# The first weight's scale is made behind its last decode, ahead of the first rows' transposes, with idle products in front of both

## The chip, the core and the metric

One core of a Trainium2 chip. The metric is the device time of one execution in microseconds, from runs of the whole program; a profiled execution comes with a trace of every instruction. Engines: PE (TensorE, products), PEld (its weight loads), DVE (VectorE), ACT (ScalarE), POOL (GpSimd), SP (SyncE, which issues the DMAs).

## The reference, cut to what matters

```
A  = softmax(q @ k_lm.T / 8);  Bm = softmax(q_lm @ k_lm.T / 8);  C = softmax(q_lm @ k.T / 8)
Z  = 6 Newton steps from Bm.T / (norm_1 * norm_inf):  Z = 2 Z - Z @ Bm @ Z
x  = A @ Z @ C @ v                      # 8 batches, 8 heads, 576 rows, head 64; 32 landmarks
u  = x + real(fft over rows and columns of x)          # per batch 576 x 512
un = (u - mean(u)) / sqrt(var(u) + 1e-6)
out = u + relu(un @ w_ch1) @ w_ch2       # w_ch1 512 x 2048, w_ch2 2048 x 512
```

## The kernel before

The last line of the reference is nearly all the work. Rows go through it in 18 chunks of two tiles of 128 rows. Both weights and the rows are held as pairs of half-precision numbers (a high and a low part), and each product takes three products of halves (`mm3`). In a chunk, eight steps multiply the transposed rows `unT` with two pieces of 128 columns of the first weight each (tile `h`, 24 products of 256 columns), ACT and DVE rectify and split the result, and eight `second` steps multiply that with the second weight into `acc` (12 products of 512 columns each).

Before this can begin, `weights` (line 275) makes the weights ready. They come as 64-bit numbers, in 16 pieces per weight (`NF = 16`), the first weight's ahead of the second's. Per piece: a DMA on SP's queue (`raw`); ACT takes the magnitudes (`prepare`, tile `row`); DVE or ACT takes the low bits and DVE puts both together (the decode, `w<-row,w`); PE adds the piece's squares to a gram matrix in the bank `acc1` (`squares`, four products). When all 16 are in, `scale` makes one power of two for the whole weight: DVE takes the gram matrix's diagonal (`wd`) and its sum (`wm`), PE spreads that over the partitions with a product against ones, DVE bounds it (`wp_e`), POOL raises it to the power -1/2 (`wp_r`), and DVE cuts and inverts it and writes the scale (`wsc`). Only then can `halve` split a piece into halves: ACT the high part, DVE the low part (both `w<-w,wsc`), two pieces after each decode (`PACE = 2`). In step i of the loop over the 32 pieces the squares of piece i - 2 are issued, so those of piece 15 come with decode 17, and `scale(0)` behind it (line 354). It takes one of the four `at` banks and waits in the plan until one is read out (`till(a2, banks=1)`). The second weight's scale comes behind decode 31.

The order of PE's instructions is made by a planner at build time. `run` (line 991) keeps a clock `now` and steps through threads: attention and mix of a batch first, then the weights, then the products of the chunks. Each thread says how long it wants to wait, from costs and due times that the kernel keeps for DVE, ACT and POOL. PE runs strictly in the planned order; while the plan has nothing for it and no chunk's second half has begun, it puts in idle products of 256 columns into `acc0` (`self.spare`, line 1015). The other engines' instructions are ordered by the compiler's scheduler, with the program's order as priority, and each of them runs its list in order.

The first batch's rows come out of `mix` (two tiles at a time) and go through `norm` (line 849): statistics, the power on POOL, the normalised rows (tile `row`), then, for the first four tiles, transposes on PE (line 248) into an `at` bank, and ACT and DVE split them into `unT`. In the plan before, the first two tiles' transposes and the second mix's products stand ahead of the first scale's product.

Of the kernel before, what the change touches and what calls it, by code (L numbers as in the profile page):

```python
# [10 lines left out]
F32 = mybir.dt.float32  # L11
# [7 lines left out]
P = 128  # L19
H, S, D, LM, DM, DF = 8, 576, 64, 32, 512, 2048  # L20
NF = DF // P
# [137 lines left out]
class Kernel:  # L159
# [80 lines left out]
    def mm(self, out, a, b, start=True, stop=True, share=1.0):  # L240
        self.there[out.name] = self.now
        self.now += share * (1.0e-3 if a.dtype == F32 else 0.42e-3) * math.prod(b.shape[1:])
        self.nc.tensor.matmul(out, a, b, start=start, stop=stop, skip_group_check=True)  # L243

    def tr(self, out, a, ident):
        self.there[out.name] = self.now
        self.now += 0.11
        self.nc.tensor.transpose(out, a, ident)  # L248
# [26 lines left out]
    def weights(self):  # L275
        nc = self.nc
        V, A = self.V, self.A
        whole = self.whole
        slots = [[t[:, OFF + 512 * i : OFF + 512 * i + 512] for i in range(NF)] for t in whole]
        upper = [[t.bitcast(BF16).rearrange("p (m x) -> p m x", x=2)[:, :, 1] for t in ss] for ss in slots]  # L280
        hl = [[t[:, 512 * i : 512 * i + 512].bitcast(F16).rearrange("p (y m) -> p y m", y=2) for i in range(NF)] for t in whole]
        self.w1s = [t.rearrange("p y (c f) -> p y c f", c=KT) for t in hl[0]]
        self.w2s = hl[1]
        sc = self.cp.tile([P, 3], F32, name="wsc")
        pieces = [(w, f) for w in range(2) for f in range(NF)]
        mags = []

        def prepare(i):


            mag = self.row(512)
            top = self.wraw[i].rearrange("p (m x) -> p m x", x=2)[:, :, 1].bitcast(F32)
            A.late = self.raw_there[i]
            A.activation(mag, top, AF.Prelu, scale=2.0**-112, alpha=-(2.0**32))
            mags.append(mag)

        def squares(i):

            w, f = pieces[i]
            for c in range(KT):  # L300
                x = upper[w][f][:, P * c : P * c + P]
                self.mm(self.gram[:, P * w : P * w + P], x, x, i == 0 and c == 0, f == NF - 1 and c == KT - 1)

        es = []

        def scale(w):

            dg, a2 = self.small(P, "wd"), self.small(1, "wm2")
            V.tensor_tensor(dg, self.gram[:, P * w : P * w + P], self.ident, ALU.mult)
            V.tensor_reduce(a2, dg, AX.X, ALU.add)  # L310
            yield self.till(a2, banks=1)
            ps = self.psum()
            self.mm(ps[:, 0:1], self.ones, a2)
            e, r = self.small(1, f"wp{w}_e"), self.small(1, f"wp{w}_r")
            V.tensor_scalar(e, ps[:, 0:1], 2.0**-120, 2.0**126, ALU.max, ALU.min)
            self.G.tensor_tensor(r, e, self.mhalf[:, 0:1], ALU.pow)
            V.tensor_scalar(r.bitcast(I32), r.bitcast(I32), 0x7F800000, None, ALU.bitwise_and)
            V.reciprocal(e, r)
            es.append(e)
            V.tensor_scalar(sc[:, w : w + 1], r, (2.0**12, 2.0**14)[w], None, ALU.mult)  # L320

        def halve():
            w, f = pieces[sum(self.split_w)]
            self.split(hl[w][f][:, 0], hl[w][f][:, 1], slots[w][f], sc[:, w : w + 1])
            self.split_w[w] = f + 1

        for i, (w, f) in enumerate(pieces):
            while len(mags) < min(2 * NF, i + 1 + PREP):
                j = len(mags)
                while len(self.wraw) < min(2 * NF, j + 1 + AHEAD):  # L330
                    self.raw()
                if self.raw_there[j] > self.now:
                    if j > i:
                        break
                    yield self.raw_there[j] - self.now
                    continue
                prepare(j)
            low = self.wraw[i].rearrange("p (m x) -> p m x", x=2)[:, :, 0]
            x, dst = mags[i].bitcast(I32), slots[w][f].bitcast(I32)
            (A if i % 2 else V).late = self.raw_there[i]  # L340
            if i % 2 == 0:
                V.tensor_scalar(dst, low, 29, None, ALU.logical_shift_right)
            else:
                byte = self.wraw[i].bitcast(mybir.dt.uint8).rearrange("p (m x) -> p m x", x=8)[:, :, 3]
                A.activation(dst, byte, AF.Copy, scale=2.0**-5, bias=-0.484375)
            V.scalar_tensor_tensor(dst, x, 3, dst, ALU.logical_shift_left, ALU.bitwise_or)
            if i > 1:
                squares(i - 2)
            self.decoded = i + 1
            if self.decoded == 2 * NF:  # L350
                self.load(1)
            yield max(0.0, max(self.V.free, self.G.free) - self.now - WT)
            if i == NF + 1:
                yield from scale(0)
            for _ in range(PACE if es else 0):
                if self.split_w[0] < NF:
                    halve()
                    yield max(0.0, max(self.V.free, self.G.free) - self.now - WT)
        squares(2 * NF - 2)
        yield 0.0  # L360
        squares(2 * NF - 1)
        yield from scale(1)
        V.tensor_scalar(sc[:, 2:3], es[0], 2.0**-25, es[1], ALU.mult, ALU.mult)
        self.inv2 = sc[:, 2:3]
        while sum(self.split_w) < 2 * NF:
            halve()
            yield max(0.0, max(self.V.free, self.A.free) - self.now - WT)
# [481 lines left out]
    def norm(self, b, uts):  # L849
        nc, V = self.nc, self.V  # L850
        n = len(uts)
# [29 lines left out]
        for j, ut in enumerate(uts):  # L881
            i = self.ntile
            while i // TCH >= self.first_done + NT - (1 < i // TCH < 4):
                yield 0.5
            self.ntile += 1
            self.utiles.append(ut)
            if i % TCH == 0:
                self.unT.append(
                    self.wk.tile([P, 1024], I32, name="unT", bufs=NT).bitcast(F16).rearrange("p (y c t) -> p y c t", y=2, c=KT)
                )  # L890
            unT = self.unT[-1]
            at = P * (i % TCH)
            if i < 2 * TCH:
                yield self.till(uns[j], banks=1) + (LATER if i >= TCH else 0.0)
                ps = self.psum()
                for c in range(KT):
                    self.tr(ps[:, P * c : P * c + P], uns[j][:, P * c : P * c + P], self.ident)
                self.split(*(unT[:, y, :, at : at + P] for y in range(2)), ps.rearrange("p (c t) -> p c t", c=KT), 1.0)
                self.ready.append(self.now + self.till(unT))
                yield 0.0  # L900
                continue
            hl = self.row(1024, F16).rearrange("p (y d) -> p y d", y=2)
            self.A.copy(hl[:, 0], uns[j])
            (self.G if b > 1 else V).tensor_tensor(hl[:, 1], uns[j], hl[:, 0], ALU.subtract)
            for y in range(2):
                nc.sync.dma_start_transpose(unT[:, y, :, at : at + P], hl[:, y])
            self.there[unT.name] = self.there[hl.name] + 4.0
            self.ready.append(self.now + self.till(unT))
            yield 0.0
# [81 lines left out]
    def run(self):  # L991


        self.ntile, self.utiles, self.unT, self.ready = 0, [], [], []
        self.ulive, self.ufree, self.first_done, self.seconds, self.folded = 0, [], 0, 0, -1
        self.split_w, self.decoded = [0, 0], 0
        self.threads = []
        self.spawn(self.attention(), 1)
        self.spawn(self.weights(), 2)
        self.spawn(self.mlp(), 3)  # L1000
        with self.tc.manual_schedule(engines={mybir.EngineType.PE}):
            while self.threads:
                for th in self.threads:
                    if th[1] <= self.now:
                        try:
                            wait = next(th[2])
                            th[1] = self.now + wait
                        except StopIteration:
                            self.threads.remove(th)
                        break  # L1010
                else:

                    until = min(t[1] for t in self.threads)
                    while self.spare is not None and until - self.now > 0.25:
                        self.mm(self.spare[:, 0:256], self.ones16, self.idle)
                    self.now = until
                assert self.now < 5000
# [67 lines left out]
```

## Time and profile before

| | us |
|---|---|
| median of three runs | 994.53 |
| lowest and highest | 993.15, 995.64 |
| the profiled execution | 993.68 |
| its span, first to last instruction | 991.9 |
| PE busy in it | 955.5 |
| DVE busy | 593.3 |
| ACT busy | 319.4 |
| mean granted TensorE clock | 0.986 |

Engines run at the same time, so the busy times don't add up. The weights are made ready and the first batch computed in the first 130 us; from there to the end PE multiplies rows with weights nearly without a pause. Where the profile gives only a helper's line (138 for DVE, ACT and POOL, 243 for products), the tiles' names tell operations apart.

### The profile page before, as it was taken

The numbers are of one execution on the slowest core, as the hardware profiler recorded it, in microseconds if no ns is written. First come the engines' busy times: TensorE is split into PE (matmuls) and PEld (weight loads), VectorE is DVE, ScalarE is ACT, GpSimd is POOL, SyncE is SP. The second block draws the span as 40 slices with busy tenths as digits, with TensorE's granted clock in tenths as the row PEclk, the third lists the DMA queues.
The fourth block names the chain that finished last, engine by engine and source line by source line (L and its number), as shares of the span: only waits on it lengthen the run. The fifth ranks groups of instructions, "written<-read, shape, count | busy, mean of one in ns | idle before, by whom it ended". The sixth has DMA issues, their size and how long they took to land.

```text
span 991.9 us, 20749 instructions
## 1 busy us (share of the span) xinstructions
PE 955.5 (96%) x8700; PEld 664.2 (67%) x8700; DVE 593.3 (60%) x1593; ACT 319.4 (32%) x652; POOL 119.0 (12%) x124
## 2 busy tenths in 40 slices
PE   6869999899999999999999999999999999999998
PEld 4648656667666777676666776676766777666665
DVE  7989797796467635396467736784634835141111
ACT  5559653243214322143214322432213412120110
POOL 0000000023021301032012301150110401010000
PEclk8889999999999999999999999999999999999999
DMA  9854204135121511025112321134111301020000
GB/s 332 292 212 150 65 2 172 37 59 154 49 44 42 149 55 23 22 58 154 44 44 42 99 104 43 23 61 172 22 33 33 52 1 42 16 40 22 1 22 22
DMA packets 97774, 74.66 MB, mean 75 GB/s; under 512 B 68112, under 2 KB 86544, under 8 KB 97552
## 3 DMA queue, kind: packets, MB, share of 16 engines
q1 hardware_dynamic: 97680, 73.34, 25.6%
q8 instruction: 68, 1.11, 0.5%
q14 instruction: 26, 0.21, 0.1%
HBM read 48.02 MB, written 9.44 MB: 58 GB/s over the span
## 4 chain that ended last, share of the span: by engine, by line
PE 86%; DVE 9%; DMA 2%; ACT 2%; issue 1%; POOL 0%; SPq 0%; DVEq 0%; ACTq 0%; POOLq 0%
PE h L243 36%; PE acc L243 35%; PE at L243 14%; DVE w L138 2%; DVE u L138 1%; DVE lm L138 1%; DVE mid L138 1%; DVE row L138 1%; DMA big<-k_dram 1%; PE at L248 1%; DMA big<-v_dram 1%; ACT w L138 0%; DMA out_dram<-u 0%; ACT row L138 0%; ACT mid L138 0%
## 5 line engine op out<-in xcount | busy, mean ns | idle before, releaser
L243 PE MATMUL h<-unT,w 128*128 128x256 f16 x3456 | 411.2, 273 | 3.8 <-DMA unT<-row 1.7
L243 PEld LDWEIGHTS <-w 128*128 128x128 f16 (+1 forms) x3584 | 344.9, 99 | 79.9 <-DVE w L138 7.3
L243 PE MATMUL acc<-w,h 128*128 128x512 f16 x1632 | 381.6, 380 | 2.7 <-DVE w L138 2.2
L243 PEld LDWEIGHTS <-h 128*128 128x128 f16 x1632 | 157.2, 99 | 162.6 <-issue 6.3
L138 DVE SCALAR_TENSOR_TENSOR h<-h 128x512 f16<-128x512 f32 x136 | 93.6, 688 | 224.8 <-ACT h L138 224.6
L138 ACT ACTIVATE h<-h 128x512 f16<-128x512 f32 x136 | 80.9, 595 | 321.8 <-PE h L243 315.7
L138 POOL TENSOR_TENSOR r<-ve,mhalf 128x2 f32<-128x2 f32 (+1 forms) x20 | 13.3, 667 | 476.6 <-DVE ve L138 472.2
L138 POOL TENSOR_TENSOR mid<-mid 128x640 f16<-128x640 f32 (+2 forms) x36 | 48.7, 1365 | 161.1 <-ACT mid L138 123.7
L138 DVE TENSOR_REDUCE lm<-big 128x32 f32<-128x576 f32 (+1 forms) x48 | 44.5, 940 | 2.8 <-DMA big<-k_dram 2.5
L243 PEld LDWEIGHTS <-big 128*128 128x128 f16 (+1 forms) x864 | 40.1, 103 | 8.1 <-issue 1.9
L138 ACT CAST row<-row 128x512 f16<-128x512 f32 (+1 forms) x40 | 20.8, 552 | 63.9 <-DVE row L138 63.9
L138 POOL TENSOR_TENSOR row<-row 128x512 f16<-128x512 f32 (+1 forms) x33 | 35.4, 1089 | 39.6 <-ACT row L138 37.7
L243 PEld LDWEIGHTS <-mid 64*128 64x128 f16 (+1 forms) x624 | 29.3, 95 | 14.8 <-issue 8.2
L138 DVE SCALAR_TENSOR_TENSOR u<-at,scw,w 128x128 f32<-128x128 f32 (+3 forms) x105 | 33.8, 389 | 5.8 <-PE at L243 4.1
L138 DVE SCALAR_TENSOR_TENSOR u<-acc,wsc,u 128x512 f32<-128x512 f32 x36 | 26.9, 748 | 12.3 <-PE acc L243 12.0
L138 DVE SCALAR_TENSOR_TENSOR w<-at,scw,w 128x262 f32<-128x262 f32 (+1 forms) x42 | 19.1, 485 | 25.2 <-ACT w L138 25.2
L243 PE MATMUL at<-mid,big 128*128 128x262 f16 (+1 forms) x288 | 32.6, 282 | 0.0
L138 DVE TENSOR_TENSOR E<-at,mask 128x256 f32<-128x256 f32 x48 | 20.1, 419 | 17.9 <-PE at L243 17.9
L243 PEld LDWEIGHTS at<-RE,E 128*128 128x128 f32 x192 | 26.6, 194 | 5.0 <-DVE big L138 1.6
L243 PE MATMUL at<-RE,E 128*128 128x64 f32 (+1 forms) x192 | 29.0, 275 | 0.2 <-DVE RE L138 0.2
L138 DVE SCALAR_TENSOR_TENSOR big<-big,aq_r 128x1024 f16<-128x1024 f32 (+1 forms) x32 | 26.8, 868 | 3.5 <-ACT big L138 3.5
L138 DVE TENSOR_TENSOR mid<-mid 128x256 f32<-128x256 f32 (+2 forms) x52 | 28.6, 584 | 0.0
(179 smaller groups left out, 897.8 us busy)
## 6 DMA issues: line engine op xcount, KB each, us to landing
w<-w_dram SPq DMA_DIRECT2D x22, 512.0 KB, 6.8
big<-v_dram SPq DMA_DIRECT2D x16, 640.0 KB, 9.5
big<-q_dram SPq DMA_DIRECT2D x16, 584.0 KB, 6.7
big<-k_dram SPq DMA_DIRECT2D x16, 576.0 KB, 5.4
out_dram<-u SPq DMA_DIRECT2D x36, 256.0 KB, 2.0
big<-w_dram SPq DMA_DIRECT2D x10, 512.0 KB, 6.5
t<-t_dram SPq DMA_DIRECT2D x1, 1048.0 KB, 10.7
unT<-row SPq DMA_TRANSPOSE x64, 2.4
```

The costliest lines, as they stand in the source:

```text
L138: ins = call(out, *args, **kw)
L243: self.nc.tensor.matmul(out, a, b, start=start, stop=stop, skip_group_check=True)
L248: self.nc.tensor.transpose(out, a, ident)
```

## The change

It adds `warm(n)`, which issues n idle products without moving the planner's clock. The squares of pieces 14 and 15 are issued right behind decode 15, with 24 idle products ahead of those of piece 15, and `scale(0)` follows at once, ahead of decode 16. Its product takes a bank of the `h` pool, its wait in the plan is only for the diagonal's sum, and eight idle products follow it. The transposes in `norm` are not issued before that (`self.scaled`). Decodes 16 and 17 no longer issue squares, and the splits begin behind piece 15. Nothing changes for the second weight's scale.

```diff
--- before.py
+++ after.py
@@ -242,6 +242,10 @@
         self.now += share * (1.0e-3 if a.dtype == F32 else 0.42e-3) * math.prod(b.shape[1:])
         self.nc.tensor.matmul(out, a, b, start=start, stop=stop, skip_group_check=True)
 
+    def warm(self, n):
+        for _ in range(n):
+            self.nc.tensor.matmul(self.spare[:, 0:256], self.ones16, self.idle, start=True, stop=True, skip_group_check=True)
+
     def tr(self, out, a, ident):
         self.there[out.name] = self.now
         self.now += 0.11
@@ -297,6 +301,8 @@
         def squares(i):
 
             w, f = pieces[i]
+            if i == NF - 1:
+                self.warm(24)
             for c in range(KT):
                 x = upper[w][f][:, P * c : P * c + P]
                 self.mm(self.gram[:, P * w : P * w + P], x, x, i == 0 and c == 0, f == NF - 1 and c == KT - 1)
@@ -308,9 +314,12 @@
             dg, a2 = self.small(P, "wd"), self.small(1, "wm2")
             V.tensor_tensor(dg, self.gram[:, P * w : P * w + P], self.ident, ALU.mult)
             V.tensor_reduce(a2, dg, AX.X, ALU.add)
-            yield self.till(a2, banks=1)
-            ps = self.psum()
+            yield self.till(a2, banks=1) if w else max(0.0, self.there[a2.name] - self.now)
+            ps = self.psum() if w else self.ps_h.tile([P, 512], F32, name="h")
             self.mm(ps[:, 0:1], self.ones, a2)
+            if w == 0:
+                self.warm(8)
+            self.scaled = True
             e, r = self.small(1, f"wp{w}_e"), self.small(1, f"wp{w}_r")
             V.tensor_scalar(e, ps[:, 0:1], 2.0**-120, 2.0**126, ALU.max, ALU.min)
             self.G.tensor_tensor(r, e, self.mhalf[:, 0:1], ALU.pow)
@@ -344,13 +353,16 @@
                 byte = self.wraw[i].bitcast(mybir.dt.uint8).rearrange("p (m x) -> p m x", x=8)[:, :, 3]
                 A.activation(dst, byte, AF.Copy, scale=2.0**-5, bias=-0.484375)
             V.scalar_tensor_tensor(dst, x, 3, dst, ALU.logical_shift_left, ALU.bitwise_or)
-            if i > 1:
+            if i > 1 and not NF <= i < NF + 2:
                 squares(i - 2)
             self.decoded = i + 1
             if self.decoded == 2 * NF:
                 self.load(1)
             yield max(0.0, max(self.V.free, self.G.free) - self.now - WT)
-            if i == NF + 1:
+            if i == NF - 1:
+                squares(NF - 2)
+                yield 0.0
+                squares(NF - 1)
                 yield from scale(0)
             for _ in range(PACE if es else 0):
                 if self.split_w[0] < NF:
@@ -890,6 +902,8 @@
                 )
             unT = self.unT[-1]
             at = P * (i % TCH)
+            while not self.scaled:
+                yield 0.1
             if i < 2 * TCH:
                 yield self.till(uns[j], banks=1) + (LATER if i >= TCH else 0.0)
                 ps = self.psum()
@@ -993,7 +1007,7 @@
 
         self.ntile, self.utiles, self.unT, self.ready = 0, [], [], []
         self.ulive, self.ufree, self.first_done, self.seconds, self.folded = 0, [], 0, 0, -1
-        self.split_w, self.decoded = [0, 0], 0
+        self.split_w, self.decoded, self.scaled = [0, 0], 0, False
         self.threads = []
         self.spawn(self.attention(), 1)
         self.spawn(self.weights(), 2)
```

## Rows read from the trace of the kernel before

**Rows 1.** From the page: busy time of each engine (share of the span) and instructions; the TensorE clock that was granted, in tenths, in 40 slices of 24.8 us; and one group of DMA issues (count, size of one, median us from issue to landing).

```profile
PE 955.5 (96%) x8700; PEld 664.2 (67%) x8700; DVE 593.3 (60%) x1593; ACT 319.4 (32%) x652; POOL 119.0 (12%) x124
...
PEclk8889999999999999999999999999999999999999
...
w<-w_dram SPq DMA_DIRECT2D x22, 512.0 KB, 6.8
```

**Rows 2.** Busy time by stretch (us from the span's start). Columns: stretch, its length, then busy us and instructions of PE, PEld, DVE, ACT and POOL, the granted TensorE clock, the mean busy share of the DMA engines, GB/s. The stretches were chosen around the change; the one from 62.1 overlaps others.

```profile
50.00:62.70 12.70, 7.77 (x100) 5.51 (x100) 11.82 (x30) 8.93 (x18) 0.02 (x1) 1.00 0.82 318
62.70:64.80 2.10, 0.00 (x0) 0.00 (x0) 2.03 (x8) 0.00 (x0) 0.69 (x1) 0.63 0.47 131
64.80:70.00 5.20, 5.16 (x25) 4.24 (x26) 2.67 (x5) 2.23 (x4) 0.00 (x0) 0.50 0.38 154
73.50:76.90 3.40, 3.40 (x21) 2.54 (x19) 3.03 (x8) 3.40 (x8) 0.00 (x0) 0.50 0.47 137
85.60:108.50 22.90, 22.09 (x233) 19.47 (x233) 21.14 (x38) 17.95 (x32) 0.00 (x0) 1.00 0.61 205
62.10:108.50 46.40, 40.98 (x385) 34.72 (x386) 39.86 (x88) 33.02 (x60) 1.96 (x3) 0.89 0.42 139
108.50:126.80 18.30, 16.00 (x95) 8.96 (x96) 14.90 (x26) 10.72 (x18) 0.55 (x1) 1.00 0.01 1
126.80:200.00 73.20, 69.11 (x703) 45.79 (x703) 57.66 (x176) 28.39 (x63) 3.87 (x5) 0.98 0.24 73
200.00:992.00 792.00, 785.97 (x6987) 541.63 (x6984) 426.87 (x1143) 210.74 (x435) 111.90 (x109) 1.00 0.21 55
```

**Rows 3.** PE in order of time, 50 to 130 us. Columns: start, us (from the first start to the last end of the merged products), engine, line, operation, out<-in, shapes, count, and in brackets the idle time before and what ended it. acc<-w are gram products, acc<-idle,ones idle products, h<-unT,w products of the rows with the split first weight, acc<-w,mid and acc<-w,h products with the split second weight.

```profile
53.61 1.52 PE L243 MATMUL at<-mid,big 128*128 128x262 f16 x12
...
62.18 0.40 PE L243 MATMUL acc<-w 128*128 128x128 bf16 x4 [2.77 <-DVE w L138]
...
64.84 1.94 PE L248 MATMUL at<-ident,row 128*128 128x128 f32 x8 [2.15 <-DVE row L138]
66.57 2.83 PE L243 MATMUL at<-mid,big 128*128 128x262 f16 x12
...
69.62 0.43 PE L243 MATMUL at<-wm,ones 128*128 128x1 f32 x2
...
73.24 3.39 PE L243 MATMUL h<-unT,w 128*128 128x256 f16 x16 [0.42 <-DVE w L138]
...
81.81 2.78 PE L243 MATMUL h<-unT,w 128*128 128x256 f16 x24
...
85.64 0.82 PE L243 MATMUL h<-unT,w 128*128 128x256 f16 x6 [0.82 <-DVE mid L138]
...
92.43 0.60 PE L248 MATMUL at<-ident,row 128*128 128x128 f32 x4
...
110.01 0.28 PE L243 MATMUL at<-wm,ones 128*128 128x1 f32 x2
...
126.78 3.59 PE L243 MATMUL acc<-w,h 128*128 128x512 f16 x11 [2.23 <-DVE w L138]
```

**Rows 4.** DVE in order of time, 60 to 81 us, the same columns. w<-row,w is a decode, wd and wm the gram matrix's diagonal and its sum, row<-u,mv,r the two row normalisations, unT<-at,unT the low part of a transposed row tile, wp_e the first reader of the scale's product, wsc the scale, w<-w,wsc the low part of a split.

```profile
61.46 0.66 DVE L138 SCALAR_TENSOR_TENSOR w<-row,w 128x512 int32<-128x512 int32 x1
...
63.57 0.28 DVE L138 TENSOR_REDUCE wm<-wd 128x1 f32<-128x128 f32 x1
...
64.14 1.00 DVE L138 TENSOR_SCALAR row<-u,mv,r 128x512 f32<-128x512 f32 x2
...
66.59 0.69 DVE L138 SCALAR_TENSOR_TENSOR unT<-at,unT 128x512 f16<-128x512 f32 x1 [0.51 <-ACT unT L138]
67.44 0.69 DVE L138 SCALAR_TENSOR_TENSOR unT<-at,unT 128x512 f16<-128x512 f32 x1 [0.16 <-ACT unT L138]
70.08 0.16 DVE L138 TENSOR_SCALAR wp_e<-at 128x1 f32<-128x1 f32 x1 [1.94 <-PE at L243]
...
71.47 0.14 DVE L138 TENSOR_SCALAR wsc<-wp_r 128x1 f32<-128x1 f32 x1
...
72.43 0.74 DVE L138 SCALAR_TENSOR_TENSOR w<-w,wsc 128x512 f16<-128x512 f32 x1
...
78.36 0.69 DVE L138 SCALAR_TENSOR_TENSOR mid<-h,mid 128x512 f16<-128x512 f32 x1 [0.79 <-ACT mid L138]
...
80.04 0.16 DVE L138 TENSOR_TENSOR rt<-r 128x2 f32<-128x2 f32 x1 [0.81 <-POOL r L138]
```

**Rows 5.** DVE in order of time, the second weight's scale and its tenth split, the same columns.

```profile
111.42 0.13 DVE L138 TENSOR_SCALAR wsc<-wp_r 128x1 f32<-128x1 f32 x1
...
125.98 0.74 DVE L138 SCALAR_TENSOR_TENSOR w<-w,wsc 128x512 f16<-128x512 f32 x1
```

**Rows 6.** ACT in order of time, the same columns: the eviction of the first transposed row tile, the rectification of one first-weight product (u<-h), and the magnitudes of the last piece (row<-big).

```profile
65.96 0.60 ACT L138 ACTIVATE unT<-at 128x512 f16<-128x512 f32 x1 [5.00 <-PE at L248]
...
105.96 0.60 ACT L138 ACTIVATE u<-h 128x512 f16<-128x512 f32 x1 [2.72 <-PE h L243]
106.45 0.67 ACT L138 ACTIVATE row<-big 128x512 f32<-128x512 f32 x1
```

**Rows 7.** The DMA queue SP, the last two issues of the second weight's pieces, in order of time.

```profile
84.10 5.44 SPq L391 DMA_DIRECT2D w<-w_dram  x2
```

## The prediction

> **What bounds the kernel now.** I read the page first. TensorE (PE) is busy 955.5 of 991.9 us, and the clock digits are below 9 only in the first three slices of 24.8 us [rows 1]. Then the busy time by stretch [rows 2]. From 200 us on PE is busy 785.97 of 792.00 us, and from 126.8 to 200 it is 69.11 of 73.20. So nothing this change touches can be won there except by starting earlier. The holes are ahead of that. Between 62.7 and 64.8 PE does nothing; from 64.8 to 70.0 it is busy but at a granted clock of 0.50, which is 1.2 GHz; likewise from 73.5 to 76.9 [rows 2].
>
> Third, PE's own order of time [rows 3]. The last four products of the first weight's gram matrix (piece 15) wait 2.77 us for their decode and run at 62.18. The transposes of the first rows wait 2.15 us and start at 64.84. Twelve products of the first batch's second mix follow, 2.83 us at half clock, where the same twelve took 1.52 at 53.61. Only behind them, at 69.62, stands the scale's product. VectorE (DVE) shows that it could have run earlier [rows 4]: its operand, the reduced diagonal, is ready at 63.57 + 0.28 = 63.85. So it lies 5.8 us behind other work in PE's queue. Its reader on DVE starts at 70.08 after 1.94 us of idling, the scale is written at 71.47 + 0.14 = 71.61, and the first product on split weights runs in earnest at 73.24.
>
> Last, who sets the end of that stage. From 62.1 to 108.5 DVE is busy 39.86 of 46.40 us; from 85.6 to 108.5 PE is busy 22.09 of 22.90 [rows 2]. PE's product at 85.64 waits for DVE [rows 3]; DVE, with ScalarE (ACT), is late up to there, and PE carries the rest. ACT's rectification at 105.96 waits 2.72 us for PE, and the second weight's last magnitude stands right behind it at 106.45 [rows 6]. That leads to the second scale at 111.42 and to its tenth split at 125.98 [rows 5], for which PE waits until 126.78 [rows 3]. A shift of the stage's first half therefore reaches 126.78, and from there PE is nearly full.
>
> **The change, part by part.**
>
> *Gram products and 24 idle ones.* Pieces 14 and 15 are squared in the step of decode 15, no longer two decodes later in the plan. On the chip nothing changes in when they can run: 62.18 waits for decode 15, which ends at 61.46 + 0.66 = 62.12 [rows 3, 4]. The idle products lie between the two. At full clock a product of 256 columns costs 0.11 us (24 in 2.78 at 81.81), so 24 take 2.6 us and fit in the 2.77 us of waiting: nothing. If the cover were gone they would cost 2.6, or at half clock (16 in 3.39 at 73.24, 0.21 each) 5.1.
>
> *The scale's chain.* Diagonal ready at 63.85, product at 63.9. For the rest I take the second weight's scale, whose chain is undisturbed: product at 110.01, scale written at 111.42 + 0.13 = 111.55, so 1.54 us [rows 3, 5]. That gives 65.4. DVE takes its work in order and may have the two row normalisations (64.14, 1.00 us) in front of the reader: then 66.2 [rows 4]. Before it was 71.61. The scale's bank is now one of the two that the first-weight products use; it is read by 65, long before the second such tile needs it: nothing.
>
> *Eight idle products* stand between the scale's product and the transposes: 63.9 + 0.28 + 0.87 = 65.05 instead of 64.84, so 0.2 us lost. With the clock kept, the eight transposes cost 0.9 (four in 0.60 with the drain at 92.43, against eight in 1.94) and the twelve products 1.4 to 1.5: done at 67.4 instead of 69.4.
>
> *First product on split weights.* It needs the transposed rows (an eviction of 0.60 each on ACT [rows 6], a low part of 0.69 each on DVE) and pieces 0 and 1 split (0.74 each on DVE). The first row's transposes end at 65.5, its eviction on ACT at 66.1, and then DVE has 0.69 + 0.69 + 0.74 + 0.74 = 2.9 us in order [rows 4]: 69.0. The ends are 68.2, if a split fills DVE's wait for ACT, and 70.0, if a decode (0.66) or the mix's additions go first. Before: 73.24. With 16 products at 0.11 instead of 0.21 (1.6 us) and a half-clock stretch that need not come back for the next few, PE could be 4.2 + 1.6 = 5.8 us earlier in this stage.
>
> *The splits move ahead of decodes 16 and 17.* Two are issued per decode, now from piece 15 on. It is the same DVE and ACT work in another order, so up to the last decode DVE can be earlier only by idling less. It idles 46.40 - 39.86 = 6.54 us. Of this 1.94 (scale's reader), 0.51 and 0.16 (rows' eviction), 0.79 (rectification) and 0.81 (the POOL power) lie where splits can now fill in [rows 4]: 4.21 us. The rest, 2.3 us, are waits for PE and the gram matrix at the stage's end, and I leave them. DVE's 4.2 is less than PE's 5.8, so DVE decides: **4.2 us**, bounded below by 1.94 (only the scale's own wait) and above by 6.54.
>
> *Queues.* The second weight's last loads leave SP at 84.10 and within 5.44 us of it [rows 7], with 6.8 us to landing at the median [rows 1], each once a decode has freed its place. Four more splits of 0.74 ahead of those decodes (3.0 us) against 4.2 us recovered leave them about 1 us earlier: nothing. POOL has only the rows' power in the way, whose reader chain is through by 64.14 [rows 4]: nothing.
>
> *The sum.* The profiled execution took 993.68 us, 1.8 over its span and 0.85 under the median of 994.53. 993.68 - 4.2 = 989.5, on the median's footing **990.3**. A measurement of this kernel tells about 0.3% (3 us) from no change.
>
> **Rivals.**
>
> *A, the clock is lost all the same.* PE still waits from 62.6 to 63.9 and again near 68 for rows and splits, and before the change the clock fell at 63 and once more by 73.5, behind such stretches [rows 2, 3]. Price: 1.3 us on the twelve products and about 1 us on the first products; of 4.2 us about 2 are left: 992.4. The Trainium skill ("TensorE: Matmul & The Clock Gate", Part 1) says that the gate's windows run free of the kernel, so that the place of a transition differs between runs; by that rule a fixed count of idle products need not hold the clock in every run. The trace of one run can't show that.
>
> *B, the gain is given back.* Every order behind this point is planned afresh. If the second weight's scale or its splits keep their place (DVE has 14.90 busy of 18.30 us from 108.5 to 126.8 [rows 2]), PE just waits longer than 2.23 us at 126.78. That gives 994.5, no change. Against it: all of that chain hangs on PE's products of the first rows, which move.
>
> *C, slower: the idle products run at half clock.* 24 then take 5.1 us from 59.3 to 64.4, the gram ends 2.2 us late, and eight more take 1.7: transposes at 67.9 instead of 64.84, and the mix's products end at 67.9 + 1.94 + 2.83 = 72.7 instead of 69.4. Of these 3.3 us one split (0.74), done by then, comes back: 2.5 us over, 997.0. It decides once the clock falls before 59.3. Against it: up to 62.7 the clock granted is 1.00 over 12.7 us [rows 2].
>
> **How the numbers follow.** Forecast 0.60 (its own range 988 to 992), A 0.13, B 0.17, C 0.10. Faster by over 3 us (below 991.6): nine tenths of the forecast, a little of A, 0.56. Slower (above 997.5): most of C, a little of B, 0.10. The rest, 0.34, is no change. The range goes from the 6.5 us that DVE could give, 987.5 with some luck in the new order, to beyond B, 995.2.
>
> **What would show it.** Right: the scale's product at about 64 and the scale written by 66.2; clock 1.00 from 62.7 to 70; twelve mix products in 1.5 us; first split product by 70; DVE idling about 2.3 us up to the last decode; second scale near 107.2 and the wait that ended at 126.78 ending near 122.6; PE after that as full as before. Wrong: if DVE still idles 5 us or more there (step of the splits), if the second scale stays at 111 (B), or if the stretch behind 126.8 gains idle time that the new plan made.

## The result, and the profile after

The change makes the kernel **slower**: median 1003.93 us (1001.25 to 1007.67, four runs) against 994.24 of the kernel before on the same chip, ratio 1.0098 with a 95% interval of 1.0076 to 1.0120. The forecast was 990.3. The profiled execution after took 1002.75 us, its span is 1000.8, the mean granted clock 0.988 (0.986 before). So the clock is no worse on the whole, and the time is lost all the same.

The stretches that answer to [rows 2], kernel after, the same columns:

```profile
62.70:64.80 2.10, 1.80 (x17) 1.15 (x15) 2.01 (x8) 0.00 (x0) 0.17 (x1) 1.00 1.02 412
64.80:70.00 5.20, 4.06 (x34) 3.38 (x35) 3.61 (x14) 2.21 (x5) 1.41 (x2) 1.00 0.05 19
...
108.50:126.80 18.30, 16.18 (x76) 7.55 (x74) 15.18 (x28) 10.90 (x17) 0.56 (x1) 0.91 0.00 1
126.80:200.00 73.20, 65.27 (x657) 42.89 (x656) 53.14 (x167) 25.32 (x59) 3.88 (x5) 0.93 0.21 68
200.00:992.00 792.00, 787.05 (x7012) 543.68 (x7007) 428.74 (x1148) 213.47 (x439) 110.44 (x109) 1.00 0.21 54
```

The front is as forecast: PE runs from 62.7 on at a granted clock of 1.00, where it had 0.63 and 0.50. (The 0.91 from 108.5 to 126.8 costs some 1.4 us, 47 products with the second weight in 12.10 us where 48 took 10.91, but the wait that ends this stretch takes it up: 0.27 us instead of 2.23.) From 126.8 to 200, however, PE is busy 65.27 us, not 69.11, and at 0.93, not 0.98. There the time is lost.

PE in the kernel after, in order of time, which answers to [rows 3]:

```profile
61.09 2.78 PE L247 MATMUL acc<-idle,ones 128*128 128x256 bf16 x24
64.12 0.41 PE L243 MATMUL acc<-w 128*128 128x128 bf16 x4 [0.25 <-DVE w L138]
...
65.78 0.38 PE L243 MATMUL h<-wm,ones 128*128 128x1 f32 x2 [1.04 <-DVE wm L138]
66.03 1.03 PE L247 MATMUL acc<-idle,ones 128*128 128x256 bf16 x8
66.97 1.09 PE L252 MATMUL at<-ident,row 128*128 128x128 f32 x8
67.89 1.52 PE L243 MATMUL at<-mid,big 128*128 128x262 f16 x12
```

The whole stage stands 1.94 us later in this execution than in the profiled one of before: the squares of piece 14 (up to there both kernels run the same instructions) start at 60.84, not 58.90. With that taken off, each of these lines is where the prediction had it. Most of the delay is the clock's. DVE's decodes of the two executions lie 0.4 to 0.6 us apart up to 43 us and 1.95 from 47 on, and between these PE's granted clock differs. In both kernels, 42 to 45 us, before and then after:

```profile
42.00:45.00 3.00, 3.00 (x39) 2.40 (x38) 2.80 (x10) 1.12 (x3) 0.00 (x0) 1.00 0.35 101
```

```profile
42.00:45.00 3.00, 3.00 (x23) 2.12 (x21) 1.85 (x5) 0.31 (x2) 0.00 (x0) 0.50 0.21 53
```

In the execution of before, the clock had been at 0.50 from 33 to 39 us and was back by then; in the one of after it was 1.00 up to 39 and fell behind that. So the same code can meet the fall at another place in another execution. This agrees with the rule cited under rival A (the Trainium skill, "TensorE: Matmul & The Clock Gate", Part 1, that the gate's windows run free of the kernel). In the twelve profiled executions of this study piece 14's squares start between 58.90 and 63.73, so **a start is taken off wherever two traces are compared below**.

Now the place of the loss. What PE waited for from 126 to 245 us (sum, number, longest), before and then after:

```profile
PE acc L243 <- DVE w L138: 2.2, 1, 2.2
PE acc L243 <- DVE u L138: 1.9, 2, 1.4
PE h L243 <- DMA unT<-row: 1.7, 1, 1.7
```

```profile
PE at L243 <- DVE nrm L138: 2.5, 2, 1.4
PE at L243 <- DVE RE L138: 2.3, 1, 2.3
PE acc L243 <- DVE u L138: 1.9, 1, 1.9
PE at L243 <- ACT mid L138: 1.7, 1, 1.7
```

The wait for the tenth split, which ended the stage before, is nearly gone (0.3 us after), and so is one of 1.7 us for transposed rows. In its place stand waits for the second batch's attention: `RE` is a Newton step, `nrm` and `mid` are parts of the same computation. The stretches in which they lie, before and then after:

```profile
144.00:150.00 6.00, 5.09 (x73) 3.35 (x70) 5.85 (x16) 2.52 (x6) 1.05 (x1) 1.00 0.01 3
150.00:156.00 6.00, 5.53 (x35) 3.72 (x35) 5.13 (x14) 1.76 (x6) 1.45 (x2) 1.00 0.73 245
156.00:162.00 6.00, 6.00 (x46) 4.29 (x45) 4.01 (x11) 1.95 (x4) 0.00 (x0) 1.00 1.03 388
```

```profile
144.00:150.00 6.00, 3.11 (x38) 2.41 (x37) 4.95 (x16) 2.18 (x5) 1.32 (x2) 0.79 0.00 0
150.00:156.00 6.00, 4.98 (x18) 2.75 (x17) 3.29 (x10) 1.73 (x6) 1.18 (x2) 0.50 0.12 45
156.00:162.00 6.00, 4.07 (x18) 2.05 (x17) 5.14 (x12) 1.45 (x3) 0.00 (x0) 0.85 0.01 3
```

The clock stays at 1.00 through PE's first hole, up to 147, and is at 0.50 from 148 to 157. PE itself in these 20 us, before and then after:

```profile
146.34 2.75 PE L243 MATMUL acc<-w,h 128*128 128x512 f16 x12
150.47 0.81 PE L243 MATMUL acc<-w,u 128*128 128x512 f16 x3 [1.37 <-DVE u L138]
...
157.42 2.78 PE L243 MATMUL h<-unT,w 128*128 128x256 f16 x24
```

```profile
147.15 0.80 PE L243 MATMUL at<-RE,E 128*128 128x64 f32 x4 [2.30 <-DVE RE L138]
148.53 1.11 PE L252 MATMUL at<-ident,mid 128*128 128x128 f32 x4 [0.59 <-POOL mid L138]
149.44 2.76 PE L243 MATMUL acc<-w,h 128*128 128x512 f16 x6
...
155.09 2.77 PE L243 MATMUL acc<-w,h 128*128 128x512 f16 x6
...
161.49 4.04 PE L243 MATMUL acc<-w,u 128*128 128x512 f16 x18 [1.93 <-DVE u L138]
165.37 0.82 PE L243 MATMUL h<-unT,w 128*128 128x256 f16 x6
```

The twelve `acc<-w,h` products are the first chunk's last `second` step (step 7). Before, they stand together at 146.34, between Newton products. After, PE waits for `RE` with nothing in front of it to do, then runs six of them at half clock at 149.44 and six at 155.09. DVE's two additions that close the chunk and free its two `acc` banks (`u<-acc,wsc,u`), before and then after:

```profile
149.67 0.74 DVE L138 SCALAR_TENSOR_TENSOR u<-acc,wsc,u 128x512 f32<-128x512 f32 x1
...
150.63 0.73 DVE L138 SCALAR_TENSOR_TENSOR u<-acc,wsc,u 128x512 f32<-128x512 f32 x1
```

```profile
153.40 0.74 DVE L138 SCALAR_TENSOR_TENSOR u<-acc,wsc,u 128x512 f32<-128x512 f32 x1
...
160.69 0.74 DVE L138 SCALAR_TENSOR_TENSOR u<-acc,wsc,u 128x512 f32<-128x512 f32 x1
```

The next chunk's `acc<-w,u` waits for the second one, until 161.49. The second chunk's fifth product step, at 157.42 before, starts at 165.37, and from 300 us to the end the additions that close the chunks come 8.4 to 9.8 us later than before, mostly 8.9.

**Where this order comes from.** PE alone runs in the planner's order. The planner's clock, printed while each kernel is built, says when the thread of the weights gave each split its turn:

| in the plan, us | before | after |
|---|---|---|
| fourth `second` step done | 111.33 | 109.71 |
| the second batch's DVE work comes | behind split 13 | behind split 12 |
| split 14 has its turn | 115.60 | 126.80 |
| `second` step 7 done | 131.00 | 134.96 |
| fifth product step of the second chunk asked | 137.41 | 140.12 |

The second batch waits in the plan for four finished `second` steps (`while b == 1 and self.seconds < NF // 2 - HB`, in two places of its attention). These come 1.6 us earlier, one split earlier than before. The batch then adds some 9 us of planned work to DVE (in the kernel after its planned end goes from 113.5 to 122.8, split 13 included), and the last loop of `weights` waits, behind each split, until DVE is nearly free (`max(self.V.free, self.A.free)`). So split 14 has its turn 11 us later and split 15 behind it 3 us later; `second` step 7, which needs both, is done 4 us later in the plan, and PE's order has it behind and between Newton products that it stood ahead of before.

### The profile page after: what moved, and what is told of

It is laid out like the page before. It is cut to its first block, busy times and chain, and to the rows that moved or that the text cites. A ratio compares the mean times of both kernels' runs of the same rounds, so it can differ in the third digit from the quotient of the medians.

```text
span 1000.8 us, 20804 instructions
## 1 busy us (share of the span) xinstructions
PE 959.4 (96%) x8726; PEld 665.8 (67%) x8726; DVE 592.6 (59%) x1593; ACT 319.3 (32%) x652; POOL 118.2 (12%) x124
## 4 chain that ended last, share of the span: by engine, by line
PE 76%; DVE 3%; DMA 0%; ACT 0%; issue 0%; POOL 0%; POOLq 0%; DVEq 0%; ACTq 0%
PE acc L243 33%; PE h L243 33%; PE at L243 11%; DVE u L138 1%; DVE lm L138 1%; DMA out_dram<-u 0%; DVE h L138 0%; DVE big L138 0%; DVE row L138 0%; DVE bn L138 0%; DVE cmx L138 0%; DVE nrm L138 0%; POOL r L138 0%; ACT h L138 0%; ACT big L138 0%
## 6 DMA issues: line engine op xcount, KB each, us to landing
t<-t_dram SPq DMA_DIRECT2D x1, 1048.0 KB, 10.4
```

## The experiments

The theory, **T1**: the front gains about 4 us, and the place of split 14 in the plan loses 11 to 13 between 140 and 165 us. Rivals: **T2**, the idle products, or the clock they change, cost the time; **T3**, the splits moved ahead of decodes 16 and 17, or the scale's bank, cost it. All ran beside the kernel before, on several chips, so two of them are compared by their ratios to it. (The first batch's Newton work that some of the expectations name is the second batch's.)

**e1, split 14 along with 13**, on the kernel after:

```diff
         while sum(self.split_w) < 2 * NF:
             halve()
+            if self.split_w[1] == NF - 2:
+                halve()
```

Expected:

> The changed kernel, but split 14 of the second weight is issued right behind split 13, ahead of the first batch's Newton work instead of behind it, as the order of the kernel before has it. Everything ahead of 126 us is the same as in the changed kernel. Theory T1 (the front gains some 4 us and the place of split 14 loses 11 to 13 between 140 and 165 us): the loss goes and the gain stays, 989 to 992, against 1003.9 of the changed kernel and 994.2 of the kernel before; the wait for RE at 147 and the half clock of 150 to 156 vanish. T2 (the idle products, or the clock they change, cost the time) and T3 (the splits moved ahead of decodes 16 and 17, or the bank, cost it): nothing of theirs is touched, 1002 to 1005.

Measured: 992.01 us (990.81 to 995.8, 12 runs; before 994.09), ratio **0.9977 (0.9964 to 0.9990)**. The added `halve()` wins 12 us, and the result is faster than both kernels; the half clock of 150 to 156 is gone (1.00). PE and DVE in e1:

```profile
143.84 2.12 PE L243 MATMUL acc<-w,h 128*128 128x512 f16 x9
...
146.18 0.81 PE L243 MATMUL acc<-w,h 128*128 128x512 f16 x3
147.28 1.46 PE L243 MATMUL acc<-w,u 128*128 128x512 f16 x6 [0.29 <-DVE u L138]
...
155.70 2.78 PE L243 MATMUL h<-unT,w 128*128 128x256 f16 x24
```

```profile
128.54 1.61 DVE L138 SCALAR_TENSOR_TENSOR w<-w,wsc 128x512 f16<-128x512 f32 x2
...
138.11 0.74 DVE L138 SCALAR_TENSOR_TENSOR w<-w,wsc 128x512 f16<-128x512 f32 x1
...
146.49 0.74 DVE L138 SCALAR_TENSOR_TENSOR u<-acc,wsc,u 128x512 f32<-128x512 f32 x1
...
148.51 0.74 DVE L138 SCALAR_TENSOR_TENSOR u<-acc,wsc,u 128x512 f32<-128x512 f32 x1
```

Its first two DVE lines are splits 13, 14 and 15. In the kernel after they are these:

```profile
128.99 1.61 DVE L138 SCALAR_TENSOR_TENSOR w<-w,wsc 128x512 f16<-128x512 f32 x2
...
138.57 0.74 DVE L138 SCALAR_TENSOR_TENSOR w<-w,wsc 128x512 f16<-128x512 f32 x1
```

That is the same place in DVE's order and, with the different starts (60.38 and 60.84), the same time. So the splits were never late on the chip. What was late is only what the planner **thought** of them, and from that the order that it wrote. Most of that is PE's: step 7's last product ends at 157.86 in the kernel after and at 146.99 in e1, 10.4 us apart without the starts, and DVE takes the second closing addition 2.8 and 1.5 us behind it. These last 1.3 us are DVE's own order, which follows the program and changes with it; no run changes PE's order alone.

**e2, the mirror image**: the kernel before, with `if self.split_w[1] == NF - 2:` and a second planner wait ahead of `halve()`.

Expected:

> The mirror image: the kernel before, with nothing of the change, but split 14 of the second weight waits in the planner as the other splits do, so that it falls behind the first batch's Newton work, as in the changed kernel. T1: the loss comes alone, without the gain: 1003 to 1007, against 994.2, with waits and half clock between 140 and 165 us. T2 and T3: 993 to 996, since neither the idle products nor the early splits are there.

Measured: 998.80 us (997.54 to 1000.65), ratio 1.0045 (1.0027 to 1.0063). Slower, without any part of the change, but by 4.5 us, half of what T1 was expected to cost.

**e3, no idle products**: the kernel after with `range(0)` in `warm`.

Expected:

> The changed kernel without its 24 and 8 idle products; the planner's order of everything else is the same, since idle products don't move its clock. T1: the loss at 140 to 165 stays and the front loses some of its 4 us through the clock: 1004 to 1007. T2: the loss came with the idle products, so 990 to 999. T3: like T1, 1003 to 1007. For the front: without idle products the clock should fall behind 62 us, and the twelve products of the second mix take up to 2.8 us instead of 1.52.

Measured: 1002.59 us (1001.47 to 1005.22), ratio 1.0083 (1.0065 to 1.0101). T2 falls; T1's range began 1.4 us higher. As expected, the clock falls behind 62 us without them: the twelve products of the second mix take 2.82 us.

**e4, splits as late as before**: in the kernel after, `for _ in range(PACE if es and i > NF else 0)`.

Expected:

> The changed kernel, but the splits begin two decodes later, where the kernel before begins them; the early scale, its bank and the idle products stay. In this plan split 14 of the second weight comes ahead of the first batch's Newton work again. T1: the loss goes, and the front keeps the part of its gain that the scale alone gives: 990 to 994. T2: 1002 to 1005. T3: the loss goes too, 990 to 996; so this run tells T2 from the others and the first of this call tells T1 from T3.

Measured: 992.84 us (990.43 to 994.66, 12 runs), ratio 0.9978 (0.9965 to 0.9991). With e1, which keeps the early splits and is as fast, T3 falls: the early splits cost only through the plan.

The next four price the idle products and turn the same order by other handles.

**e5, e1 without idle products.**

Expected:

> The changed kernel with split 14 right behind split 13 (992.0 in the first call) and without the 24 and 8 idle products: what the idle products are worth where the loss at 140 to 165 us is absent. Theory P (they keep the clock, and the front stands on that): the profiles of the changed kernel with and without them differ by some 1.6 us at the fifth to tenth product step of the first chunk, once the start of the stage is taken off, so 993 to 994.5. Theory Q (DVE decides the front, the clock of PE there is covered): 991 to 992.7, the same as with them.

Measured: 995.02 us (991.84 to 997.5, 12 runs), ratio 1.0006 (0.9990 to 1.0021). Against e1 the idle products are worth 0.29% (some 0.2 either way, by the two intervals), 2.9 us. That speaks for P by the size, with the median 0.5 above P's range, but the traces don't show P's reason: without the starts, e5 is 0.4 us behind e1 at the second chunk's fourth product step, and 2.3 at 206 us, behind a stretch at a clock of 0.78 (192 to 198 us) where e1 has 1.00.

**e6, idle products alone**: the kernel before with `self.warm(24)` ahead of piece 15's squares.

Expected:

> The kernel before with one part of the change alone: 24 idle products in front of the first weight's last gram products; scale, transposes and splits stay where they were. P: the clock of the eight transposes and the twelve products of the second mix is kept (1.3 us less for the products, about 1 for the transposes), 992 to 993. Q: the scale's product still stands behind the mix, but its reader on DVE is what counts; 993.5 to 995. Idle products by themselves as the cause of the loss of the changed kernel: 1000 or more.

Measured: 992.56 us (990.5 to 996.68, 12 runs), ratio 0.9986 (0.9970 to 1.0001). The median is in P's range, but the interval holds no change as well.

**e7, the second batch later**: the kernel after with `NF // 2 - HB + 1` in both waits, nothing else.

Expected:

> The changed kernel, with the other handle on the same order: nothing is done to the splits, but the second batch's two waits in the planner ask for one more finished second half of the first chunk (five, not four). In this plan splits 13 to 15 come ahead of the second batch's work and the last second half is planned for 121.1 us instead of 135.0. T1, sharpened (on the chip DVE has the splits in the same order in both; it is the order written for PE that changes, in which the last second half of the first chunk and the next steps come 4 to 6 us late, so that nothing stands between the Newton products of the second batch): 988 to 992. If the loss hangs on something else than that order, on the early start of the second batch as such or on the early splits: 998 to 1004.

Measured: 995.06 us (991.95 to 999.1, 12 runs), ratio 1.0003 (0.9986 to 1.0020). Some 9 us of the loss go by a change that touches neither splits nor scale; 3 more than T1 allowed stay. In its trace the two closing additions stand at 138.61 and 140.72, and PE waits elsewhere: 1.5 us for `mid`, 1.2 for `RE`, and 3.1 near 310 us for an addition that itself waits for an output write.

**e8, splits 14 and 15 along**: e1 with a third `halve()`.

Expected:

> The changed kernel with splits 14 and 15 both issued right behind 13: the last second half is then planned for 122.4 us, against 129.4 with split 14 alone and 135.0 in the changed kernel, and all later steps 0.6 us earlier than with split 14 alone. T1: 989 to 992, no slower than the 992.0 with split 14 alone. Rival: DVE's burst for the second batch is delayed by another split (0.74 us each) and PE waits for it: 993 to 996.

Measured: 993.23 us (991.9 to 996.56, 12 runs), ratio 0.9991 (0.9978 to 1.0003). The loss is gone here too. The median lies in the rival's range, not in T1's, but the interval overlaps e1's.

The last two go after the size that e2 missed.

**e9, filler held**: in the kernel after, the second chunk's fourth product step also waits for `ch == 1 and i == 3 and self.split_w[1] < NF - 1`.

Expected:

> The changed kernel with split 14 left where it is, but the fourth product step of the second chunk (24 products of rows with the first weight) held in the planner until split 14 has had its turn, so that PE's written order puts it among the Newton products of the second batch instead of ahead of them. Why: holding split 14 in the kernel before cost only 4.7 us, where undoing it in the changed kernel won 11.9. If the rest is that in the changed kernel PE has used up its fillers before the Newton products (its waits and half-clock stretches of 144 to 158 us are empty of products of rows), 996 to 999.5: part of the loss goes, the last second half is still late. If only the place of split 14 counts: 1002 to 1005, as the changed kernel.

Measured: 1003.61 us (999.41 to 1005.99, six runs; before 996.2 on this chip), ratio 1.0074 (1.0051 to 1.0097). The interval overlaps that of the kernel after and only touches what the filler theory wanted (996 to 999.5 is up to 1.0053 of 994.2): not shown by the times. The 24 products do stand among the Newton products now (18 at 146.18 and 6 at 148.54). The second closing addition comes at 159.06, and PE waits 3.9 us for it; but this execution starts late (63.73), and without the start that is 4.5 us earlier than in the kernel after. The trace keeps 3.2 us of this up to the additions near 308 us and loses it right behind them, where DVE waits 3.04 us for an output write, against 1.06 in the kernel after, and the clock falls:

```profile
320.28 0.99 DVE L138 SCALAR_TENSOR_TENSOR u<-at,scw,w 64x256 f32<-64x256 f32 x3 [3.04 <-DMA out_dram<-u]
```

So one trace speaks for the filler theory, and the times don't.

**e10, e4 with split 14 held**, as in e2.

Expected:

> The changed kernel with splits that begin two decodes later (992.8 as it was, with split 14 ahead of the second batch's work) and split 14 held by one wait of the planner, as it was held in the kernel before, where that cost 4.7 us, and not the 11.9 that undoing it won in the changed kernel. T1: the last second half is planned for 134.0 us, not 130.3; the second of DVE's two additions that close the first chunk comes at 158 us or later, not at 147, and the time is over 996 in either case. If the price of that place is the same in every front, 996.5 to 999; if the early scale makes it dearer (all else ahead is earlier and still waits for the same products), 1001 to 1005. Below 995: T1 has to fall.

Measured: 995.13 us (993.76 to 998.71, 12 runs), ratio 1.0020 (1.0006 to 1.0034). Against e4 that is 0.42%, 4.2 us, as in e2 (4.5). It is slower by the held split alone, but less than expected: the second closing addition comes at 154.03, not 158, and the median lies below each range that was given, 0.13 above the line where T1 had to fall (the kernel before ran at 993.3 beside it).

```profile
154.84 5.73 PE L243 MATMUL acc<-w,u 128*128 128x512 f16 x18 [2.03 <-DVE u L138]
```

So where the splits begin late, the place of split 14 costs 4 to 5 us, and where they begin early, 12 (1.0098 against 0.9977). In the single traces, with the starts taken off, the last closing additions put it at 5.1 us (e10 against e4) and 9.5 (the kernel after against e1), twice as much. Why it is dearer there **stays open**. Early splits move the second batch's work ahead of split 13 too, and less stands between the Newton products; e9, which put products back there, won 3.2 us by its trace up to 308 us and nothing in its times.

## Why the prediction was wrong, step by step

**The front was right**, nearly term by term. Starts taken off, in us:

| kernel | squares of piece 14 | second chunk's fourth product step | shift | less the start |
|---|---|---|---|---|
| before | 58.90 | 138.32 | | |
| after | 60.84 | 136.22 | -2.10 | **-4.04** |
| e1 | 60.38 | 135.77 | -2.55 | **-4.03** |
| e4 | 59.09 | 134.47 | -3.85 | **-4.04** |
| e3, no idle products | 59.26 | 135.86 | -2.46 | -2.82 |
| e5, no idle products | 63.28 | 139.11 | +0.79 | -3.59 |
| e6, idle products alone | 60.84 | 137.82 | -0.50 | -2.44 |
| e2, the front of before | 63.33 | 141.56 | +3.24 | -1.19 |

e2 shows how far such a figure can be off: its front is that of the kernel before, yet it comes out 1.19 us shorter. Its clock was back at one place where that of the kernel before was at 0.50. The 16 products that stand at 73.24 in [rows 3], 3.39 us, are these in e2:

```profile
76.94 1.92 PE L243 MATMUL h<-unT,w 128*128 128x256 f16 x16 [0.42 <-DVE w L138]
```

- *DVE's 4.2 us at the stage's end*: from the end of decode 15 to the end of the last decode it is 46.28 us before and 42.05 after, 4.23 less, and DVE idles 2.62 us of it, not 6.44 (forecast 2.3). At the second chunk's fourth product step it is 4.04 in three executions, against one execution of the kernel before; against e2's front it would be 2.85. Whether the two halves of the change add up (2.44 by the idle products, 2.8 to 3.6 by the early scale, 4.04 by both) can't be told within 1.2 us.
- *24 idle products cost nothing*: 2.78 us, and 0.25 of the wait is left. *Eight cost 0.2*: the transposes start at 66.97, 0.19 behind 64.84 + 1.94.
- *Clock kept*: eight transposes in 1.09 (forecast 0.9), twelve products in 1.52. Rivals A and C, both about the clock in the front, came about in none of the seven profiled executions that have both the early scale and the idle products: the clock is 1.00 from 60 to 80 us in each.
- *Scale by 65.4 to 66.2*: `wsc` is written at 67.62 + 0.13 = 67.75, which is 65.81 without the late start. *First split product at 69.0*: 69.57, which is 67.63; in earnest at 70.54, 68.60.
- *Second scale at 107.2*: wrong in between. It is written at 111.00 + 0.13 = 111.13, against 111.55 [rows 5], 2.4 us earlier without the start, not 4.2, though the last decode was 4.2 earlier: from 100 to 110 us PE works through gram products and products of rows without a pause, and the last gram products wait their turn. The stage made it up behind that.

**The step that failed is the carry**: "A shift of the stage's first half therefore reaches 126.78, and from there PE is nearly full." The first half of the sentence held in the main (the wait that ended at 126.78 ends at 125.95, 124.01 without the start, 2.8 us earlier). The second was read from rows of an order that the change does not keep: 69.11 busy of 73.20 us belonged to the plan before. The fourth `second` step, 1.6 us earlier in the plan, put another order behind it, and 4.0 us of gain became 9.7 of loss in the medians. The last sign of being wrong, idle time behind 126.8 that the new plan made, is the one that came: 73.20 - 65.27 = 7.9 us, against 4.1. Rival B named just this ("every order behind this point is planned afresh"), but priced it as a gain given back, 994.5, with no mechanism that could cost more than was won; so the range ended at 995.2, 8.7 us short. And the rival on the slow side was spent on the clock in the front, which [rows 2] already spoke against.

**What a cure of the order is worth** is less than the front's 4.0 us as well: 2.1 in the medians of e1, 1.3 in those of e4. In e1's trace the step that starts at 155.70 is 3.2 us early without the start (157.42 before), and at the end 2.6 are left (span 990.8 - 1.48 against 991.9). In e4's, 1.3 us go at one place near 305 us, where DVE's addition waits for an output write to free its tile. The write's issue on SP's queue and DVE's wait, in the kernel before, then in e4:

```profile
307.67 1.63 SPq L934 DMA_DIRECT2D out_dram<-u  x2
...
309.76 0.99 DVE L138 SCALAR_TENSOR_TENSOR u<-at,scw,w 64x256 f32<-64x256 f32 x3 [0.82 <-DMA out_dram<-u]
```

```profile
303.38 2.20 SPq L948 DMA_DIRECT2D out_dram<-u  x2
...
306.76 0.99 DVE L138 SCALAR_TENSOR_TENSOR u<-at,scw,w 64x256 f32<-64x256 f32 x3 [2.12 <-DMA out_dram<-u]
```

The write is issued as much earlier as all else (303.38 against 307.67); it takes longer, 3.38 us from its issue to the end of DVE's wait, not 2.09. An earlier front isn't what makes it long: in e6, 2.9 us early there without the start, it takes 2.09, in e7 4.45 and in e9, which is late, 4.31. Whether that belongs to these kernels or to the executions that were profiled isn't shown. "PE nearly full" hid a wait (0.82 us before) that can take part of a gain.

## What to carry to other kernels

Where an engine's order is planned at build time, a shift of 2 us at one gate can turn the order of work 50 us later; so before a gain is carried to the end, list the planner's waits behind the change that count events (here four `second` steps, and "DVE free" behind each split) and ask which of them opens one event earlier. Price that as a rival with a sign of its own: here the place of one split in the plan was worth 4 to 12 us, the whole intended gain 4. And compare two traces of such a kernel only after the start of the stage is taken off by an instruction that both share, and with a third trace that tells how far such a figure can be off.

## What the runs showed of the hardware

- The same instructions up to 58.9 us take up to 4.8 us longer in other executions (piece 14's squares between 58.90 and 63.73), with the granted clock's falls in other places between 30 and 60 us. The totals spread by as much, which may be the same: e1's twelve runs lie within 5.0 us, e5's within 5.7.
- Such a delay is not lost for good. e2's trace is 4.43 us late at piece 14 and only 3.24 at the second chunk's fourth product step, since its clock is 0.98 from 72 to 80 us, where that of the kernel before was 0.50 from 73.5 to 76.9.
- The same output write, issued 0.8 us behind the closing addition in each kernel, held its tile for 2.09 to 4.45 us from its issue.
